# Retention and two feed-forward layers on one core: chunk loads issued by ScalarE, x of two visits in one buffer and one store, drains in the preparation's buffers

## The chip, the core and the metric

The kernel runs on one core of a Trainium2 chip. TensorE (PE) multiplies matrices, VectorE (DVE) and ScalarE (ACT) do the elementwise work, SyncE (SP) issues the transfers (DMAs) between the memory of the chip (DRAM) and the core's own memory. The metric is the time of one execution on the device in microseconds (us), as a median of several runs.

## What is computed

Retention is attention without softmax: the scores are multiplied by a decay per head and masked to earlier positions. Its result x (2304 tokens, 512 wide) passes through two feed-forward layers of width 2048, the first with softplus, the second with a squared ReLU. All is float32.

```python
scores = scale * np.matmul(q, k.transpose(0, 1, 3, 2))
Dmat = np.where(rel >= 0, gamma[:, None, None] ** rel[None, :, :], 0.0)
x = np.matmul(scores * Dmat[None], v)            # 4 x 8 heads x 576 x 64
x = x.transpose(0, 2, 1, 3).reshape(2304, 512)
h = x @ moe_w_in                                  # first layer
x = (np.maximum(h, 0) + np.log1p(np.exp(-np.abs(h)))) @ moe_w_out
r = np.maximum(x @ moe2_w_in, 0)                  # second layer
out = (r * r) @ moe2_w_out
```

## The kernel before, in words

**Numbers as two halves.** A float32 number is split into a rounded part and the rest (names ending in h and l: `gh` and `gl`, `xh` and `xl`), and a product is made of three matrix products of such parts. So every operand costs ScalarE a cast and VectorE a subtraction.

**Stages.** The first layer handles three tiles of tokens, of 512, 384 and 384 (tile 0, 1 and 2, up to token 1280), in 16 steps each; then the other 1024 tokens in one block by Strassen's scheme (lines 1015 and 1148), then the whole second layer by the same scheme (lines 697 and 770) up to the end of the kernel. The change is in the tiles and in the drains.

**A step** (`step`, one of 16 blocks f of the hidden width) does, in this order: g1, 12 matmuls into a PSUM bank `ph` (line 558); Softplus of the bank on ScalarE into `e` (line 569); one or more visits of the retention (`attend`, in tiles 1 and 2 one per step for as long as there are visits); the split of the step before (`split_g`: `gh` on ScalarE, `gl` on VectorE, lines 576 and 577); the rest of the visit (`rest`, called `later()` in `step`); g2 of the step before that, 12 matmuls into four `acc` banks (line 592); then a share of the preparation of the second layer's weights (`pump_step`).

**A visit** works on 64 tokens. Two visits (s = 0 and 1) share a chunk c, which lies in one of the two halves of the buffer `ring`: q and k (0.5 MB), and k and v by tokens (0.5 MB). TensorE makes the scores `pb` of the new chunk (line 426), the outputs `po` of the old one (line 474) and the running state `st` (line 451). VectorE masks `pb` into the ring (line 436) and scales v (line 407), ScalarE copies the state (line 462), VectorE scales `po` into x (line 505 for the tiles, line 497 for tokens from 1280 on).

**The loads of chunks.** `visit` with s = 1 frees one half of the ring: the outputs of the old chunk c - 1 are its last readers. `load_chunk(c + 1)` then issues two DMAs (line 397), first q and k, then k and v. The visit of the next step needs q and k of that chunk for its scores. All these loads, the weights' loads (lines 141 and 146), the stores of prepared weights (`s2d`, line 237), of the first layer's weights (`wod`, line 1581), of x (`x1d`, line 500) and of the results (`x2d`, line 603) stand in one row on SyncE's queue, in the order of the program, and each waits there for what it reads or overwrites.

**Buffers.** Tag `l` of the pool `ew` has two buffers, shared by x of tokens from 1280 on, by two of the four copies of a drain (`drain_one` with odd j, on VectorE) and later by other values. Tag `ct` of the pool `cvt` has six buffers; the preparation writes its words and halves there and stores them from there, and the other two copies of a drain (on ScalarE) take them too. A drain copies the four `acc` banks after the last step of a tile, and stores them.

Up to the end of the tiles the order of the instructions on each engine is that of the program; behind it a scheduler orders them. The result of a visit, x, is 128 x 256 values, 128 KB.

Of the kernel before, what the change touches and what calls it, by code (L numbers as in the profile page):

```python
# [7 lines left out]
F32 = mybir.dt.float32  # L8
# [4 lines left out]
ALU = mybir.AluOpType  # L13
# [3 lines left out]
P = 128  # L17
D = 64
CN = 64
# [9 lines left out]
BLOCK = 1280  # L29
# [25 lines left out]
def kernel(  # L55
# [26 lines left out]
    nc = tc.nc  # L82
# [6 lines left out]
    KD = DM // P  # L89
# [10 lines left out]
    cvt = ctx.enter_context(tc.tile_pool(name="cvt", bufs=6))  # L100
    xs = ctx.enter_context(tc.tile_pool(name="xs", bufs=1))
    ew = ctx.enter_context(tc.tile_pool(name="ew", bufs=2))
# [25 lines left out]
    x1d = dram.tile([2 * FULL // CN, P, KD * CN], F32, name="x1d")  # L128
# [227 lines left out]
    def pump_begin(upto):  # L356
        while n_split[0] < min(n_one, upto):
# [6 lines left out]
            n_used[0] += count  # L364
            begun.append(made)

    x_raw = {}
    chunk = {}
    xop = {}
# [11 lines left out]
    def tile_of(token):  # L381
        for t, (t0, n) in enumerate(TILES):
            if t0 <= token < t0 + n:
                return t, token - t0
        raise ValueError(token)
# [3 lines left out]
    def new_chunk(c):  # L389
        s = c % LOADS * 4  # L390
        chunk[c] = ring[:, s:s + 4].rearrange("p i (h c) -> p i h c", c=CN)

    def load_chunk(c):
        if c < NPR:
            new_chunk(c)
            for i, src in ((0, qk_t), (2, kv)):
                nc.sync.dma_start(
                    out=chunk[c][:, i:i + 2],
                    in_=src[2 * c:2 * c + 2].rearrange("s p i h c -> (s p) i h c"),
                )  # L400

    def scale_v(c):
        if c < NPR:
            t = chunk[c][:, 3]
            m = 2 * c % SCH
            w = vw[:, m * H:(m + 1) * H]
            nc.vector.tensor_tensor(
                out=t, in0=t, in1=w.unsqueeze(2).to_broadcast([P, H, D]), op=ALU.mult
            )
# [6 lines left out]
    def turn(c, s):  # L416
        return (2 * c + s) % SCH, (LO, HI)[s]

    def scores(c, s, pb):
        _, rows = turn(c, s)  # L420
        qp, kk = (chunk[c][rows, i] for i in range(2))
        tos = ((LO, HI), (HI, LO))[s]

        def pair(h):
            for to, hh in zip(tos, (h, h + HH)):
                nc.tensor.matmul(  # L426
                    pb[to, h, :], lhsT=kk[:, hh, :], rhs=qp[:, hh, :],
                    start=True, stop=True, skip_group_check=True,
                )
        return [lambda h=h: pair(h) for h in range(HH)]  # L430


    def masked(c, s, pb):
        _, rows = turn(c, s)
        for i, of in enumerate(((LO, HI), (HI, LO))[s]):
            nc.vector.tensor_tensor(  # L436
                out=chunk[c][rows, 1, i * HH:(i + 1) * HH], in0=pb[of], in1=mask[of], op=ALU.mult
            )

    def states(c, s):  # L440
        m, rows = turn(c, s)
        if m == SCH - 1:
            return []
        if m == 0:
            state[:] = [ps_st.tile([P, HH, D], F32, tag="st", name="st")]
        st = state[0]
        kk, sv = (chunk[c][rows, i] for i in (2, 3))

        def pair(h):
            for to, hh in ((LO, h), (HI, h + HH)):  # L450
                nc.tensor.matmul(
                    st[to, h, :], lhsT=kk[:, hh, :], rhs=sv[:, hh, :],
                    start=m == h == 0, stop=True, skip_group_check=True,
                )
        return [lambda h=h: pair(h) for h in range(HH)]

    def next_state(c, s):
        m, _ = turn(c, s)
        if m < SCH - 1:
            to = (HI, LO)[s]  # L460
            for of, i in ((LO, 0), (HI, 1)):
                nc.scalar.copy(before[to, i * HH:(i + 1) * HH], state[0][of])

    def outputs(c, s, po, carried_first=True):
        m, rows = turn(c, s)
        qp, pp, sv = (chunk[c][rows, i] for i in (0, 1, 3))
        parts = (True, False) if carried_first else (False, True)
        todo = [
            (h, carried) for carried in parts if m or not carried for h in range(0, H, 2)
        ]  # L470

        def pair(n, h, carried):
            for hh in (h, h + 1):
                nc.tensor.matmul(  # L474
                    po[(LO, HI)[hh % 2], hh // 2, :],
                    lhsT=before[rows, hh, :] if carried else sv[:, hh, :],
                    rhs=qp[:, hh, :] if carried else pp[:, hh, :],
                    start=(n == 0), stop=True, skip_group_check=True,
                )
        return [lambda a=a: pair(*a) for a in [(n, *t) for n, t in enumerate(todo)]]  # L480

    def rounds(lower, upper):
        for r in range(max([*lower, *upper, -1]) + 1):
            for half in (lower, upper):
                if r in half:
                    half[r]()

    def at_rounds(*lists):
        return {r0 + r: fn for r0, fns in lists for r, fn in enumerate(fns)}

    def scaled(c, s, po):
        m, _ = turn(c, s)
        token = (2 * c + s) * CN
        xw = cst[:, C_XW + m * 256:C_XW + (m + 1) * 256].rearrange("p (a b) -> p a b", a=KD)
        if token >= BLOCK:
            x = ew.tile([P, 512], F32, tag="l", name="x")[:, :KD * CN]
            nc.vector.tensor_tensor(
                out=x.rearrange("p (a b) -> p a b", a=KD), in0=po, in1=xw, op=ALU.mult
            )
            nc.sync.dma_start(out=x1d[(token - BLOCK) // CN], in_=x)  # L500
            return
        t, off = tile_of(token)
        if t not in x_raw:
            x_raw[t] = xs.tile([P, 512 // CN, KD, CN], F32, tag="xr", name="xr")
        nc.vector.tensor_tensor(out=x_raw[t][:, off // CN], in0=po, in1=xw, op=ALU.mult)
# [29 lines left out]
    def h_bank(name, turn=True):  # L535
        t = ps_h.tile([P, 512], F32, tag=f"h{n_h[0] % 2}", name=name)
        n_h[0] += turn
        return t

    def in_heads(t):  # L540
        return t.rearrange("p (h c) -> p h c", c=CN)
# [54 lines left out]
    def drain_one(j, src, dst, n):  # L596
        if j % 2 == 0:
            o = cvt.tile([P, 512], F32, tag="ct", name="xo")[:, :n]
            nc.scalar.copy(o, src[:, :n])
        else:  # L600
            o = ew.tile([P, 512], F32, tag="l", name="xo")[:, :n]
            nc.vector.tensor_copy(o, src[:, :n])  # L602
        nc.sync.dma_start(out=dst, in_=o)


    def drain(t0, n):
        for j in range(KD):
            drain_one(j, acc[j], x2d[j, :, t0:t0 + n], n)
# [319 lines left out]
    KB = KH * FULL  # L928
    PRODUCT_S = {1: 0, 3: 1, 4: 2, 6: 3}
    t1 = {}  # L930
    full = {}

    def full_raw(i, j):
        return ring.rearrange("p i n -> p (i n)")[:, (2 * i + j) * KB:(2 * i + j + 1) * KB]
# [456 lines left out]
    with tc.manual_schedule():  # L1391
# [12 lines left out]
        for c in range(2, last):  # L1404
            early_qk(c)
            early_kv(c)
        pump_load(3)
        load_chunk(last)
        nc.vector.memset(causal[LO, CN:], 1.0)
        nc.vector.memset(causal[HI, :CN], 0.0)  # L1410
# [69 lines left out]
    def visit(c, s):  # L1480
        old, new = c - 1 in chunk, c < NPR
        first, then = {}, {}
        if old:
            po = in_heads(ps_at.tile([P, 512], F32, tag="at", name="po"))[:, :HH]
            first = at_rounds((0, outputs(c - 1, s, po)))
        if new:
            if c == last:
                pb = in_heads(ps_at.tile([P, 512], F32, tag="at", name="pb"))[:, :HH]
            else:
                pb = in_heads(h_bank("pb", False))[:, :HH]  # L1490
            then = at_rounds((4, scores(c, 1 - s, pb)))
        if s == 0:
            if old:
                then.update(at_rounds((0, states(c - 1, 1))))
            rounds(first, then)
        else:
            if new:
                then.update(at_rounds((0, states(c, 0))))
            rounds(then, first)
        if s and old:  # L1500
            load_chunk(c + 1)
        if new:
            masked(c, 1 - s, pb)

        def rest():
            if s == 0 and old:
                next_state(c - 1, 1)
            elif s and new:
                next_state(c, 0)
            if old:  # L1510
                scaled(c - 1, s, po)
            if s == 0:
                scale_v(c)
            elif old:
                del chunk[c - 1]
        return rest
# [9 lines left out]
    def attend(b, f):  # L1526
        rest = None
        while tick[0] < visits(b, f):
            if rest:
                rest()  # L1530
            rest = visit(*divmod(tick[0], 2))
            tick[0] += 1
        return rest
# [11 lines left out]
    def step(j):  # L1545
# [23 lines left out]
        if j == 0:  # L1569
            load_chunk(last + 1)  # L1570
# [114 lines left out]
```

## Time and profile before

| | before |
|---|---|
| median of 3 runs (lowest, highest) | 831.34 us (831.02, 831.78) |
| the profiled execution, its own time | 830.39 us |
| its span, first to last instruction | 828.6 us |
| granted TensorE clock over the span | 0.994 |
| busy PE, DVE, ACT | 806.9, 653.4, 402.8 us |
| DMA issues of ring loads, line 397 | 14 of each half, 512 KB each |
| DMAs through ScalarE's queue (q10) | 0.09 MB of 202 MB |

Tiles 1 and 2 run from about 125 to about 300 us; visits end near 257 us. Views of the profile: the waits of an engine (who ended its idle time), the timeline (single instructions; "SPq" is an issue of a DMA by SyncE, "ACTq" by ScalarE), the chain that ended last, and windows (busy time, granted clock and transfers of a stretch). Idle time of an engine that nobody waits for costs nothing.

### The profile page before, as it was taken

To read this page: it belongs to the slowest core of one execution; us is meant where nothing else is said; L and a number is where in the kernel's file an instruction comes from. 1 tells how busy PE (TensorE), PEld (TensorE's weight loads), DVE (VectorE), ACT (ScalarE), POOL (GpSimd) and SP (SyncE) were. 2 spreads that over 40 slices of the span, in tenths; PEclk is the share of its full clock that TensorE was granted. 3 is DMA by queue.
4 is the path that set the end of the run, shared out by engine and by line. 5 is a ranking of instruction groups with operands and counts; after the bars stand their busy time and mean duration, and the time that the engine had idled before them with its cause. 6 is when DMAs were issued, how large, how long until landed. Compare 5 with 4: busy or idle time off the path is not lost.

```text
span 828.6 us, 16334 instructions
## 1 busy us (share of the span) xinstructions
PE 806.9 (97%) x5909; PEld 716.1 (86%) x5909; DVE 653.4 (79%) x1255; ACT 402.8 (49%) x781; POOL 0.2 (0%) x4
## 2 busy tenths in 40 slices
PE   8899999989889999999999999999999999999998
PEld 5678889978879997888888899988999988999887
DVE  4899885665755899977778698999797997787876
ACT  3888874543433565556666411464221554111553
POOL 0000000000000000000000000000000000000000
PEclk9999999999999999999999999999999999999999
DMA  9867765898856673327999887898987888877885
GB/s 228 280 185 229 229 217 160 272 317 246 287 188 220 197 233 123 96 83 276 290 330 305 288 285 251 260 311 286 298 252 247 250 271 278 284 250 249 253 272 172
DMA packets 129747, 201.97 MB, mean 244 GB/s; under 512 B 11010, under 2 KB 73090, under 8 KB 128898
## 3 DMA queue, kind: packets, MB, share of 16 engines
q1 hardware_dynamic: 129504, 200.85, 75.7%
q8 instruction: 47, 0.77, 0.4%
q14 instruction: 32, 0.26, 0.1%
q10 hardware_dynamic: 164, 0.09, 0.1%
HBM read 153.71 MB, written 47.19 MB: 242 GB/s over the span
## 4 chain that ended last, share of the span: by engine, by line
PE 80%; DMA 10%; DVE 5%; ACT 2%; issue 1%; SPq 1%; DVEq 0%; ACTq 0%
PE acc L1148 10%; PE acc L592 9%; PE py L770 9%; PE py L697 9%; PE ph L558 9%; PE pz L770 6%; PE px L770 6%; PE pz L697 6%; PE px L697 6%; DMA ring<-in_qk_t_dram 3%; PE py L1015 3%; PE pz L1015 2%; PE px L1015 2%; DMA wi_raw<-in_moe_w_in_dram 2%; PE po L474 1%
## 5 line engine op out<-in xcount | busy, mean ns | idle before, releaser
L592 PE MATMUL acc<-gh,wo 128*128 128x384 f32 (+1 forms) x384 | 118.1, 368 | 1.1 <-DVE xo L602 1.1
L697 PE MATMUL py<-t,sring 128*128 128x384 f32 x432 | 88.4, 339 | 0.7 <-DVE uring L901 0.7
L558 PE MATMUL ph<-xh,wi 128*128 128x384 f32 (+1 forms) x376 | 81.0, 357 | 2.9 <-DVE ring L436 1.5
L592 PEld LDWEIGHTS acc<-gh,wo 128*128 128x128 f32 x384 | 72.5, 192 | 8.8 <-DVE xo L602 1.4
L697 PEld LDWEIGHTS py<-t,sring 128*128 128x128 f32 x432 | 74.9, 188 | 3.7 <-DVE uring L901 1.8
L558 PEld LDWEIGHTS ph<-xh,wi 128*128 128x128 f32 x376 | 68.5, 191 | 8.7 <-issue 1.8
L592 PE MATMUL acc<-gl,wo 128*128 128x384 f32 (+1 forms) x192 | 69.3, 361 | 0.8 <-DVE gl L577 0.8
L718 DVE TENSOR_TENSOR gring<-g,gring 128x384 fp32r<-128x384 f32 (+1 forms) x100 | 57.2, 575 | 12.0 <-ACT gring L750 7.3
L750 ACT CAST gh<-g 128x384 fp32r<-128x384 f32 x84 | 43.2, 515 | 46.7 <-PE px L770 16.3
L718 DVE TENSOR_TENSOR gl<-g,gh 128x384 fp32r<-128x384 f32 (+1 forms) x100 | 57.4, 576 | 9.6 <-ACT gh L750 7.7
L750 ACT CAST gring<-g 128x384 fp32r<-128x384 f32 x84 | 43.3, 516 | 40.1 <-PE py L770 16.4
L697 PE MATMUL pz<-t,sring 128*128 128x384 f32 x288 | 58.9, 335 | 0.0
L697 PE MATMUL px<-t,sring 128*128 128x384 f32 x288 | 58.3, 335 | 0.0
L436 DVE TENSOR_TENSOR ring<-pb,cst 64x256 f32<-64x256 f32 x56 | 23.6, 422 | 42.4 <-PE pb L426 27.7
L569 ACT ACTIVATE e<-ph 128x384 f32<-128x384 f32 (+1 forms) x48 | 25.2, 525 | 64.2 <-PE ph L558 63.9
L897 ACT COPY uring<-px 128x384 f32<-128x384 f32 x24 | 11.5, 480 | 87.8 <-PE px L697 87.8
L718 DVE TENSOR_TENSOR g<-g 128x384 f32<-128x384 f32 x96 | 52.5, 554 | 1.4
L234 ACT CAST ct<-ct 128x512 fp32r<-128x512 f32 (+1 forms) x64 | 35.8, 564 | 35.0 <-DVE ct L258 12.2
L697 PEld LDWEIGHTS px<-t,sring 128*128 128x128 f32 x288 | 50.5, 188 | 0.6 <-ACT uring L897 0.5
L697 PEld LDWEIGHTS pz<-t,sring 128*128 128x128 f32 x288 | 50.8, 188 | 0.1
L235 DVE TENSOR_TENSOR ct<-ct 128x512 fp32r<-128x512 f32 (+1 forms) x64 | 39.2, 621 | 9.5 <-ACT ct L234 6.4
L1148 PE MATMUL acc<-gring,wo 128*128 128x512 f32 x192 | 44.8, 389 | 0.0
(155 smaller groups left out, 1748.5 us busy)
## 6 DMA issues: line engine op xcount, KB each, us to landing
sring<-s2d SPq DMA_DIRECT2D x168, 256.0 KB, 3.2
sring<-o2d SPq DMA_DIRECT2D x168, 256.0 KB, 3.5
wi_raw<-in_moe_w_in_dram SPq DMA_DIRECT2D x32, 512.0 KB, 4.6
wo_raw<-in_moe_w_out_dram SPq DMA_DIRECT2D x32, 512.0 KB, 4.3
s2d<-ct SPq DMA_DIRECT2D x48, 256.0 KB, 4.2
o2d<-ct SPq DMA_DIRECT2D x48, 256.0 KB, 3.3
ring<-in_qk_t_dram SPq DMA_DIRECT2D x14, 512.0 KB, 5.4
ring<-in_kv_dram SPq DMA_DIRECT2D x14, 512.0 KB, 6.4
```

What stands on the lines that cost most here:

```text
L234: nc.scalar.copy(h, src)
L235: nc.vector.tensor_tensor(out=l, in0=src, in1=h, op=ALU.subtract)
L436: nc.vector.tensor_tensor(out=chunk[c][rows, 1, i * HH:(i + 1) * HH], in0=pb[of], in1=mask[of], op=ALU.mult)
L558: nc.tensor.matmul(ph[:, :n], lhsT=a, rhs=x, start=(j == 0), stop=(j == len(todo) - 1))
L569: nc.scalar.activation(out=g, in_=hps.pop(key)[:, :n], func=AF.Softplus)
L592: nc.tensor.matmul(acc[j][:, :n], lhsT=a, rhs=x, start=(begin and m == 0), stop=(end and m == 2))
L697: nc.tensor.matmul(ps, lhsT=a, rhs=x, start=(first and m == 0), stop=(m == len(todo) - 1), skip_group_check=True,)
L718: nc.vector.tensor_tensor(out=out, in0=a, in1=b, op=ALU.subtract)
L750: nc.scalar.copy(h, src)
L770: nc.tensor.matmul(blocks[m][:, :cols], lhsT=a[:, c], rhs=x, start=(first and p == n == 0), stop=(p == NP - 1 and n == len(todo) - 1), ski ...
L1015: nc.tensor.matmul(ps, lhsT=a, rhs=x, start=(first and m == 0), stop=(m == len(todo) - 1), skip_group_check=True,)
L1148: nc.tensor.matmul(accs[half][j], lhsT=a[:, c], rhs=x, start=(begin and m == 0), stop=(end and m == 2),)
```

## The change

1. `load_chunk` takes the queue as an argument. In `visit` the call moves from behind the visit's matmuls to the head of `rest`, with `nc.scalar`: these loads (12 chunks, 24 DMAs) are issued by ScalarE, behind `gh` of the split and ahead of the copies of the state. The loads ahead of the tiles and the one in step 0 stay on SyncE.
2. x of the two visits of a chunk lies in one buffer of 128 x 2 x 256, and is stored by one DMA of 256 KB after the second visit, in place of two of 128 KB.
3. The odd copies of a drain take a buffer of `ct` in place of one of `l`.

```diff
-    def load_chunk(c):
+    def load_chunk(c, queue=nc.sync):
         if c < NPR:
             new_chunk(c)
             for i, src in ((0, qk_t), (2, kv)):
-                nc.sync.dma_start(
+                queue.dma_start(
...
         if token >= BLOCK:
-            x = ew.tile([P, 512], F32, tag="l", name="x")[:, :KD * CN]
+            if s == 0:
+                full["x"] = ew.tile([P, 2, KD * CN], F32, tag="l", name="x")
+            x = full["x"]
             nc.vector.tensor_tensor(
-                out=x.rearrange("p (a b) -> p a b", a=KD), in0=po, in1=xw, op=ALU.mult
+                out=x[:, s].rearrange("p (a b) -> p a b", a=KD), in0=po, in1=xw, op=ALU.mult
             )
-            nc.sync.dma_start(out=x1d[(token - BLOCK) // CN], in_=x)
+            if s:
+                m = (token - BLOCK) // CN - 1
+                nc.sync.dma_start(out=x1d[m:m + 2].rearrange("m p x -> p m x"), in_=x)
             return
...
         else:
-            o = ew.tile([P, 512], F32, tag="l", name="xo")[:, :n]
+            o = cvt.tile([P, 512], F32, tag="ct", name="xo")[:, :n]
             nc.vector.tensor_copy(o, src[:, :n])
...
-        if s and old:
-            load_chunk(c + 1)
         if new:
             masked(c, 1 - s, pb)
         def rest():
+            if s and old:
+                load_chunk(c + 1, nc.scalar)
             if s == 0 and old:
                 next_state(c - 1, 1)
```

In the order of SyncE, a stretch of tile 1 with the pair of ring loads issued from 178.43 us on (the next pair follows behind the last row); before:

```order
L500 DMA x1d<-x 128x256
L237 DMA s2d<-ct 128x2x256 x4
L1581 DMA wod<-wo_697 128x512
L397 DMA ring<-in_qk_t_dram 128x1024
L397 DMA ring<-in_kv_dram 128x1024
L500 DMA x1d<-x 128x256
L141 DMA wi_raw<-in_moe_w_in_dram 128x4x256
L1581 DMA wod<-wo_697 128x512
L500 DMA x1d<-x 128x256
L141 DMA wi_raw<-in_moe_w_in_dram 128x4x256
L237 DMA s2d<-ct 128x2x256 x2
L1581 DMA wod<-wo_697 128x512
```

The same stretch of SyncE after the change (line numbers are 4 or 5 higher there):

```order
L237 DMA s2d<-ct 128x2x256 x4
L1585 DMA wod<-wo_697 128x512
L505 DMA x1d<-x 128x2x256
L141 DMA wi_raw<-in_moe_w_in_dram 128x4x256
L1585 DMA wod<-wo_697 128x512
L141 DMA wi_raw<-in_moe_w_in_dram 128x4x256
L237 DMA s2d<-ct 128x2x256 x2
L1585 DMA wod<-wo_697 128x512
```

The ring loads are gone from SyncE, and the stores of x, one behind each visit, have become one per chunk, twice as large, behind the second visit.

In the order of ScalarE, the step around 176 us, before (`e` is Softplus, `ct` the preparation's casts, `ring<-st` the copies of the state):

```order
L234 CAST ct<-ct 128x512 x2
L569 ACTIVATE e<-ph 128x384
L576 CAST gh<-e 128x384
L462 COPY ring<-st 64x256 x2
L171 ACTIVATE wi_raw<-wi_raw 128x512
L172 ACTIVATE wi_raw<-wi_raw,cst 128x512
```

The same step of ScalarE after the change:

```order
L234 CAST ct<-ct 128x512 x2
L574 ACTIVATE e<-ph 128x384
L581 CAST gh<-e 128x384
L398 DMA ring<-in_qk_t_dram 128x1024
L398 DMA ring<-in_kv_dram 128x1024
L463 COPY ring<-st 64x256 x2
L171 ACTIVATE wi_raw<-wi_raw 128x512
L172 ACTIVATE wi_raw<-wi_raw,cst 128x512
```

The two loads stand behind the two casts of the preparation, Softplus and the cast to `gh`, and ahead of the copies of the state.

## Rows read from the trace of the kernel before

**Rows 1.** Waits of TensorE, 136 to 262 us: total us, times, longest us:
```profile
PE pb L426 <- DMA ring<-in_qk_t_dram: 7.6, 4, 2.7
PE ph L558 <- DVE ring L436: 1.5, 1, 1.5
PE acc L592 <- DVE xo L602: 1.1, 1, 1.1
```

**Rows 2.** Timeline of ScalarE, four Softplus: start, us, what, idle before and its releaser:
```profile
146.62 0.49 ACT L569 ACTIVATE e<-ph 128x384 f32<-128x384 f32 x1 [2.00 <-PE ph L558]
...
235.34 0.49 ACT L569 ACTIVATE e<-ph 128x384 f32<-128x384 f32 x1 [0.92 <-PE ph L558]
...
245.38 0.49 ACT L569 ACTIVATE e<-ph 128x384 f32<-128x384 f32 x1 [4.17 <-PE ph L558]
...
250.84 0.49 ACT L569 ACTIVATE e<-ph 128x384 f32<-128x384 f32 x1 [3.36 <-PE ph L558]
```

**Rows 3.** Windows: stretch, us, busy PE PEld DVE ACT POOL, PEclk, DMA share, GB/s:
```profile
196.80:200.20 3.40, 3.33 (x35) 3.25 (x36) 2.13 (x5) 0.00 (x1) 0.00 (x0) 0.50 0.68 250
241.20:244.60 3.40, 3.01 (x10) 3.04 (x11) 3.33 (x7) 0.00 (x1) 0.00 (x0) 0.51 0.78 237
```

**Rows 4.** Timeline of TensorE: last of a visit, and the next visit where it waited:
```profile
176.39 0.22 PE L474 MATMUL po<-ring 64*64 64x64 f32 x2
...
183.67 0.27 PE L426 MATMUL pb<-ring 64*64 64x64 f32 x2 [1.96 <-DMA ring<-in_qk_t_dram]
```

**Rows 5.** Chain of waits, its ring loads: issue, us to landing, what:
```profile
164.44 5.96 DMA ring<-in_qk_t_dram
178.43 5.20 DMA ring<-in_qk_t_dram
190.35 6.38 DMA ring<-in_qk_t_dram
217.63 5.54 DMA ring<-in_qk_t_dram
```

**Rows 6.** Timeline of SyncE ahead of the load of 178.43:
```profile
175.08 2.71 SPq L237 DMA_DIRECT2D s2d<-ct  x4
```

**Rows 7.** Timeline of TensorE: last of two other visits with late loads:
```profile
189.48 0.34 PE L474 MATMUL po<-ring 64*64 64x64 f32 x6
...
215.18 0.22 PE L474 MATMUL po<-ring 64*64 64x64 f32 x2
```

**Rows 8.** Timeline of ScalarE in the visits of 176 and 215 us:
```profile
175.35 0.62 ACT L234 CAST ct<-ct 128x512 fp32r<-128x512 f32 x1 [0.30 <-DVE ct L260]
176.38 0.51 ACT L576 CAST gh<-e 128x384 fp32r<-128x384 f32 x1
...
215.41 0.50 ACT L576 CAST gh<-e 128x384 fp32r<-128x384 f32 x1
```

**Rows 9.** Line 397, the ring loads: issue ns min/median/max, and us to landing:
```profile
L397 SPq DMA_DIRECT2D ring<-in_qk_t_dram x14: 328/343/2476, 15.4 to 231.0; - x14
...
DMA to landing us min/median/max: 3.3/6.0/10.6
```

**Rows 10.** Line 1397, DMAs that ScalarE issues: issue ns min/median/max:
```profile
L1397 ACTq DMA_DIRECT2D cst<-in_consts_dram x2: 554/582/611, 0.7 to 1.3; - x2
```

**Rows 11.** Windows of the stretch with ring loads, and of a full one:
```profile
164.40:231.00 66.60, 58.97 (x849) 55.23 (x850) 41.20 (x86) 28.46 (x63) 0.00 (x0) 0.95 0.85 273
166.00:175.00 9.00, 8.00 (x102) 7.55 (x101) 6.20 (x14) 2.49 (x6) 0.00 (x0) 1.00 1.01 351
```

**Rows 12.** Timeline of VectorE around 222 us:
```profile
221.94 0.69 DVE L235 TENSOR_TENSOR ct<-ct 128x512 fp32r<-128x512 f32 x1 [0.41 <-ACT ct L234]
223.95 0.43 DVE L436 TENSOR_TENSOR ring<-pb,cst 64x256 f32<-64x256 f32 x1 [1.32 <-PE pb L426]
```

**Rows 13.** Timeline of SyncE and VectorE at the drain of the second tile:
```profile
232.90 0.33 SPq L500 DMA_DIRECT2D x1d<-x  x1
...
238.67 0.56 DVE L602 COPY xo<-acc 128x384 f32<-128x384 f32 x1 [5.34 <-DMA x1d<-x]
```

More of the change, by code (lines that the diff above doesn't have):

```diff
@@ L365, in pump_begin @@
             begun.append(made)
+    full = {}
     x_raw = {}
@@ L930 @@
     t1 = {}
-    full = {}
     def full_raw(i, j):
```

## The prediction

> **What bounds the kernel now.** I read the engines' shares first: TensorE is busy for 806.9 of 828.6 us, so only its idle time and its slow time can be won. Its waits between 136 and 262 us come next [rows 1]: 7.6 us in four waits of scores `pb` for a ring load, 1.1 us for a drain's copy `xo`, 1.5 us for a mask `ring` that VectorE had not made yet. Then I looked at how steps follow each other, because a stall costs more than its idle time. ScalarE starts Softplus when `ph` is done, so in a step without a stall the distance of two such starts is the step: 250.84 - 245.38 = 5.46 us [rows 2]. From 146.62 to 245.38 us there are 15 steps in 98.76 us, where 15 x 5.46 = 81.90 would do: 16.86 us are lost. The step from 235.34 to 245.38 alone, that of the drain, takes 10.04 us, 4.58 more than a quiet one; the other 12.28 us belong to the ring loads.
>
> Of the 16.86 us, 10.2 are the waits of [rows 1]. The granted clock gives the next part: in three stretches of 3.4 us, the first and the last of which are shown, it is 0.50, the lower of the two levels, 1.2 GHz [rows 3]; half of 3 x 3.4 is 5.1 us. They begin behind a ring wait, behind the longest ring wait, and behind the two waits of the drain. The stall of 1.96 us before 183.67 us [rows 4] has no such stretch behind it. The last 1.6 us I put down to the refilling of the pipeline behind stalls.
>
> **Why the ring loads are late.** Take the load of 178.43 us. The outputs that free its half of the ring end at 176.39 + 0.22 = 176.61 us, and TensorE is ready for the new scores at 183.67 - 1.96 = 181.71 us [rows 4]: a load has 5.10 us from the last output to its landing. It took 5.20 us, was issued 1.82 us late [rows 5], and TensorE waited 1.96. It was late because SyncE worked through four stores and one more ahead of it, from 175.08 us on [rows 6]. The load of 217.63 us came 2.23 us behind its last output at 215.40, that of 190.35 us 0.53 behind 189.82 [rows 5, 7]. The load of 164.44 us was issued in time and took 5.96 us: transfers issued before it were still under way. The shortest ring load took 3.3 us [rows 9], which shows what a load needs when little lies ahead of it.
>
> **The change part by part.** *Loads on ScalarE.* Twelve chunks, 24 DMAs, leave SyncE. ScalarE reaches them behind `gh`. At 215 us `gh` ends at 215.91, so the issue comes about 0.5 us behind the last output, in place of 2.23; at 190 us it comes at once, in place of 0.53. At 176 us it is different: ScalarE's cast `ct` of 175.35 us waits for work of VectorE and writes a buffer whose store has to land, Softplus and `gh` follow and end at 176.89 us [rows 8]. With no stall before it TensorE would be there 1.3 us earlier, ScalarE not: I take the issue as 1.5 us late and a stall of 1.4 us that stays.
>
> The issue itself takes 0.34 us on SyncE in the median [rows 9] and 0.55 to 0.61 us where ScalarE issues now [rows 10]; two per chunk hold ScalarE for 0.7 to 1.2 us. Behind them wait the copies of the state, needed one step later, and the preparation. ScalarE is busy for 28.5 of 66.6 us in this stretch [rows 11] and idles 1 to 4 us before a Softplus [rows 2], so this costs nothing; without that cover it would be 0.7 to 1.2 us per chunk, 8 to 14 us for twelve.
>
> How long the loads take on a queue of their own no row shows, since ScalarE moves no large transfer before. The bounds are the rows of the ring loads: 3.3 us, with which no stall is left, and 6.38 us [rows 5, 9]. I take 4.7 us, about the middle. That leaves the 1.4 us at 176 us, about 0.4 us at the other loads together, and nothing that lowers the clock.
>
> The Trainium skill, "DMA: Bandwidth & Descriptors", section "Queues, rings and completion order", says that each DMA engine takes turns between the queues that have work for it, packet by packet. By this rule a load would pass most of what lies ahead on SyncE's queue; no row of the trace before shows it.
>
> *Cover that is late next.* From 221.94 to 222.63 us VectorE makes a half `ct`, and the mask of the visit, two of 0.43 us, comes behind it [rows 12]. Without the stall the new scores start at 215.40 + 5.10 = 220.5 and end some 0.4 us later; g1 of the next step writes the same bank behind g2, which is about 2.1 us of the 5.46 us step: at 223.0 us. The mask is done at 222.63 + 0.86 = 223.5, so TensorE waits about 0.5 us: 0.6 us stay with refilling.
>
> *Transfers.* From 164.4 to 231.0 us 273 GB/s are moved in 66.6 us, 18.2 MB [rows 11]. These are ten steps, 54.6 us without stalls: 333 GB/s, against 351 in one of the fullest stretches, where the DMA engines are busy throughout [rows 11]. So the stage comes near what the transfers can do. At 351 GB/s it fits; at 300 GB/s it would take 60.7 us, 6 us more. I take 2.0 us, and 0 and 6 as ends.
>
> *One store for two visits.* Eight stores of 256 KB replace sixteen of 128 KB; eight issues of 0.33 us [rows 13] leave SyncE, which nobody on the path waits for. The second visit's x now stands in a buffer that was already taken for the first, so VectorE waits for a store half as often. I cost it at nothing.
>
> *Drains in `ct`.* VectorE's copy `xo` waited 5.34 us for the store of x, issued at 232.90 us, and VectorE's masks stood behind it [rows 13]. With six `ct` buffers, whose last stores stand well ahead of the drain on SyncE, the copies find room. The preparation's next words wait for the drain's stores instead; these need 5.8 us if they land like that store of x (238.67 - 232.90), about when, a step later, the words are due. I keep 0.3 of 4.58 us. The scheduler orders the block behind the tiles a little differently on VectorE and ScalarE; I cost that at 0, with 1 us either way.
>
> **Sum.** Lost 16.86; still lost afterwards 1.4 + 0.4 + 0.6 + 2.0 + 0.3 = 4.7; gain 12.2. From the profiled execution's 830.4 us that gives 818.2; the median of the runs stands 0.95 above that execution, so 819.1 us.
>
> **Rivals.** *A: only the late issue is won.* If transfers take as long as before, the loads stall by their length plus lateness less 5.10: 0.9 (5.96), 1.4 (6.38 with 0.1), 1.0 (5.54 with 0.5), and at 176 us 5.20 with 1.5, 1.6; 4.9 us, with a share of refilling 5.7, perhaps one slow-clock stretch of 1.7, and the 0.6, 2.0 and 0.3 from above: 10.3 stay, gain 6.6, 824.8 us. For it: all DMAs share the same engines, full in the critical 5 us. Against it: loads that had little ahead of them took 3.3 us.
>
> The Trainium skill, same page, section "Issuing engines are not separate DMA queues", speaks for this rival: issuing from several engines saves only the time of the issue. By it the result is 824.8 us.
>
> *B: ScalarE holds the loads back, slower.* Behind its own order, with casts that wait for stores to land, ScalarE could be late at every chunk as it is at 176 us. With eight stalls of 2.2 us, 17.6 us, and four stretches of half clock at 1.7, 24.4 us stand against the 12.28 of now; less 4.3 from the drain that is 7.8 us more, 839.1 us. It decides from about 2 us on, where eight stalls alone (16.6 / 8) use up both gains. For it: the one visit at 176 us. Against it: `gh` ends within 0.5 us of the last output at 215 us, and ScalarE mostly waits for TensorE.
>
> *C: transfers bind.* At 300 GB/s 6 us of the stage stay in place of 2, and preparation that is late makes VectorE and ScalarE late at two or three more masks, some 3 us: gain 12.2 - 4 - 3 = 5.2, 826.1 us.
>
> *D: no change.* The stalls move elsewhere one for one, 831 us. Nothing in the rows speaks for it.
>
> **How the numbers follow.** Forecast 0.55, A 0.22, C 0.09, D 0.05, B 0.09. The predicted time is that of the forecast, 819.1 us. Its own range goes from 814.5 (all 16.86 won) to 823; with A and most of C the range is 814.4 to 828.0 us. A measurement of this kernel tells about 0.2% from no change. Faster by more: forecast, A and C, 0.86; within: 0.05; slower: 0.09.
>
> **What would show it.** Waits of `pb` for ring loads fall from 7.6 to about 2 us; one of them, about 1.4 us, remains near 178 us, behind an issue that comes late on ScalarE. Ring loads through ScalarE's queue take 4 to 5 us. No stretch of half clock is left between 190 and 245 us. The copy `xo` no longer waits for x. Fifteen steps from the second of tile 1 on take about 87 us in place of 98.8. Wrong I am if the loads still take 5.5 us and more, if ScalarE's `gh` ends behind the last output by 1.5 us at several chunks, or if `xo` or `ct` wait for stores instead.

## The result and the profile after

The changed kernel takes 821.3 us in the median of four runs (819.63 to 824.67) against 831.2; the ratio is 0.988, its 95% interval 0.985 to 0.990. Forecast were 819.1 us and a range from 814.4 to 828.0. The profiled execution took 819.63 us where 818.2 was forecast, 10.76 us less than that of before.

TensorE's waits between 136 and 262 us, for [rows 1]; columns: who waited for what, us in total, times, longest:

```profile
PE pb L427 <- DMA ring<-in_qk_t_dram: 5.4, 4, 2.0
PE ph L563 <- DVE ring L437: 0.9, 1, 0.9
```

Ring waits fell from 7.6 to 5.4 us only. The wait for the drain's copy and the wait of 1.5 us for a mask behind it are gone; the 0.9 us is another mask, the one that the prediction looked for near 222 us. TensorE's timeline:

```profile
222.88 1.30 PE L563 MATMUL ph<-xh,wi 128*128 128x384 f32 x6 [0.85 <-DVE ring L437]
```

ScalarE's timeline, its Softplus starts, for [rows 2]:

```profile
146.64 0.49 ACT L574 ACTIVATE e<-ph 128x384 f32<-128x384 f32 x1 [0.83 <-PE ph L563]
...
225.32 0.49 ACT L574 ACTIVATE e<-ph 128x384 f32<-128x384 f32 x1 [1.53 <-PE ph L563]
230.72 0.49 ACT L574 ACTIVATE e<-ph 128x384 f32<-128x384 f32 x1 [0.58 <-PE ph L563]
236.18 0.49 ACT L574 ACTIVATE e<-ph 128x384 f32<-128x384 f32 x1 [1.77 <-PE ph L563]
```

The drain's step, 230.72 to 236.18, is 5.46 us, a quiet step to the hundredth. The 15 steps take 236.18 - 146.64 = 89.54 us, 9.22 less than before; the other 1.5 us were won behind the tiles. Against 15 quiet steps 7.64 us are still lost. Windows of the stretch of ten steps (columns as in [rows 3]), for the first of [rows 11]:

```profile
164.40:226.41 62.01, 57.35 (x915) 53.20 (x915) 41.59 (x86) 29.59 (x64) 0.00 (x0) 1.00 0.88 294
```

The granted clock is 1.00 throughout, where it was 0.95, and the 18.2 MB pass in 62.0 us in place of 66.6. The chain of waits still has three ring loads (issue, us to landing), for [rows 5]; below it the issues of the ring loads on ScalarE (ns min/median/max), for [rows 9, 10]:

```profile
142.27 6.47 DMA ring<-in_qk_t_dram
...
165.93 6.92 DMA ring<-in_qk_t_dram
...
189.99 6.16 DMA ring<-in_qk_t_dram
```

```profile
L398 ACTq DMA_DIRECT2D ring<-in_qk_t_dram x12: 334/335/392, 74.6 to 226.4; - x12
L398 ACTq DMA_DIRECT2D ring<-in_kv_dram x12: 444/483/1232, 75.0 to 226.8; - x12
```

The wait behind the first of the three is new (first row, TensorE's timeline). The kernel before issued this load at 142.24 us, and TensorE did not wait for it (second row, its chain of waits):

```profile
148.78 0.33 PE L427 MATMUL pb<-ring 64*64 64x64 f32 x4 [1.62 <-DMA ring<-in_qk_t_dram]
...
142.24 5.00 DMA ring<-in_qk_t_dram
```

Whether the queue made it longer is looked at under parts 2 and 3 alone.

From 90 us on none of the loads was issued later than 0.1 us behind the last output, but two of the three took longer than any ring load of [rows 5]. What lay ahead of the load of 165.93 us shows in SyncE's timeline (first fence) and in the DMA queues' share of the 1.98 us behind its issue, of the next 2.09 us, and of the 0.99 us behind the issue of the load of 155.01 us, which landed after 3.3 us (second fence: queue, packets, MB, share; q1 is SyncE's, q10 ScalarE's):

```profile
164.22 0.37 SPq L141 DMA_DIRECT2D wi_raw<-in_moe_w_in_dram  x1
164.65 0.50 SPq L1585 DMA_DIRECT2D wod<-wo  x1
```

```profile
q1 hardware_dynamic: 527, 0.61, 97.6%
...
q10 hardware_dynamic: 138, 0.54, 84.0%
q1 hardware_dynamic: 59, 0.09, 22.2%
...
q1 hardware_dynamic: 10, 0.02, 4.4%
```

For two microseconds after the issue only bytes that SyncE had issued before move, 0.61 MB. The first of the two is the delay of an issue: with next to nothing ahead ScalarE's packets start after about 1 us. In the second none of them moves either. Later both queues move side by side: from 170.0 to 172.9 us, just before the load lands, they share the engines like this,

```profile
q1 hardware_dynamic: 517, 0.51, 52.3%
q10 hardware_dynamic: 144, 0.49, 46.2%
```

and SyncE's part is work that it issued from 167.80 us on, behind the load. "DMA: Bandwidth & Descriptors" of the Trainium skill, section "Queues, rings and completion order", has the engines take turns between queues packet by packet. The stretch from 170.0 to 172.9 us fits this; in the second microsecond behind the issue no packet of ScalarE's queue got a turn.

So the bytes ahead are not the whole length. The load of 202.05 us had as much ahead of it, three stores of 256 KB, and landed after 5.0 us without a wait (SyncE's timeline, and the load's KB and us to landing):

```profile
200.53 1.59 SPq L237 DMA_DIRECT2D s2d<-ct  x3
...
ring<-in_qk_t_dram ACTq DMA_DIRECT2D x1, 512.0 KB, 5.0
```

What makes the difference, the kind of transfer ahead or what SyncE issues behind, no run takes apart.

The drain's odd copies, VectorE's timeline, for [rows 13]; they wait for nothing:

```profile
228.17 1.03 DVE L607 COPY xo<-acc 128x384 f32<-128x384 f32 x2
```

### The profile page after: what moved, and what is told of

Same layout as the page of the kernel before. It is cut to its first block, busy times and chain, and to the rows that moved or that the text cites. A ratio compares the mean times of both kernels' runs of the same rounds, so it can differ in the third digit from the quotient of the medians.

```text
span 817.8 us, 16322 instructions
## 1 busy us (share of the span) xinstructions
PE 801.8 (98%) x5909; PEld 712.2 (87%) x5909; DVE 653.5 (80%) x1255; ACT 402.5 (49%) x781; POOL 0.2 (0%) x4
## 4 chain that ended last, share of the span: by engine, by line
PE 89%; DMA 6%; DVE 2%; ACT 1%; issue 1%; SPq 1%; DVEq 0%; ACTq 0%
PE acc L597 12%; PE ph L563 11%; PE acc L1152 11%; PE py L702 9%; PE py L775 9%; PE px L702 6%; PE pz L775 6%; PE px L775 6%; PE pz L702 6%; PE py L1019 4%; PE px L1019 3%; PE pz L1019 2%; DMA ring<-in_qk_t_dram 2%; PE po L475 2%; DMA qk<-in_qk_t_dram 1%; PE pb L427 1%
## 5 line engine op out<-in xcount | busy, mean ns | idle before, releaser
L597 PE MATMUL acc<-gh,wo 128*128 128x384 f32 (+1 forms) x384 | 115.9, 363 | 0.0
L597 PEld LDWEIGHTS acc<-gh,wo 128*128 128x128 f32 x384 | 70.8, 188 | 7.3 <-ACT gh L581 0.4
```

The source lines that it names most:

```text
L597: nc.tensor.matmul(acc[j][:, :n], lhsT=a, rhs=x, start=(begin and m == 0), stop=(end and m == 2))
```

## The experiments

Theory M: a ring load lands when the bytes that were issued ahead of it, on whichever queue, are through; a queue of its own saves the lateness of the issue and nothing more. Its rivals are a delay that belongs to ScalarE's queue, and the mere fullness of the DMA engines. Ratios are to the kernel before on the same chip, whose runs there spread from 828 to 838 us, more than the 0.2% that the prediction took for the noise. Waits are totals of TensorE's ring waits in one profiled execution, 136 to 262 us. That execution need not be a typical one: those of parts 2 and 3 alone (829.4 us), of the doubled stores (826.4) and of the last row (818.7) were the slowest of their kernels, that of the moved stores (818.2) the fastest of its four.

| kernel | ratio, 95% interval | ring waits us |
|---|---|---|
| the change | 0.988 (0.985 to 0.990) | 5.4 |
| the change, again | 0.987 (0.983 to 0.990) | 4.9 |
| part 1 alone | 0.993 (0.990 to 0.995) | 6.0 |
| parts 2 and 3 alone | 0.992 (0.989 to 0.994) | 10.6 |
| part 2 alone | 1.003 (1.001 to 1.005) | 10.8 |
| part 3 alone | 0.993 (0.990 to 0.995) | 8.0 |
| first half of q, k first | 0.989 (0.983 to 0.995) | 4.0 |
| weight stores out of tile 1 | 0.987 (0.981 to 0.992) | 2.1 |
| weight stores doubled | 0.990 (0.985 to 0.994) | 7.3 |
| 512 KB loads behind ring loads | 0.980 (0.977 to 0.983) | 0.2 |
| that, weight stores moved too | 0.980 (0.976 to 0.983) | 0 |
| that order, on SyncE | 0.989 (0.987 to 0.991) | 2.9 |
| that order, without part 2 | 0.980 (0.977 to 0.983) | 1.0 |

**Part 1 alone.** The drain copies and x of the kernel before, with

```diff
-        if s and old:
-            load_chunk(c + 1)
...
         def rest():
+            if s and old:
+                load_chunk(c + 1, nc.scalar)
```

> Part 1 alone: the chunk loads are issued by ScalarE in `rest`, x and the drains are as before. Theory S (the two gains are separate): the drain keeps its step of about 10 us with the 4.6 us lost there, the half clock behind it and the two waits; the ring part gives what it gave in the changed kernel, 11 - 4.6 = 6 us or so: 825 us. Rival T (the parts need each other: without the free buffers VectorE's copies and masks come late and the loads gain nothing, or the x stores in their old place lengthen the loads): under 3 us gained, 828 to 831.

825.1 us against 832.4. The ring waits are about those of the full change, and the drain's stall stands as before: VectorE's copy waits for the store of x, and half clock follows (first window). A second stretch of half clock stands behind the first ring wait, 1.65 us (second window), where the changed kernel's profile has none behind 1.62 us.

```profile
236.64 0.56 DVE L602 COPY xo<-acc 128x384 f32<-128x384 f32 x1 [5.58 <-DMA x1d<-x]
```

```profile
238.80:242.20 3.40, 2.66 (x9) 2.67 (x9) 3.32 (x8) 0.38 (x1) 0.00 (x0) 0.50 0.68 202
149.40:152.80 3.40, 3.40 (x12) 3.40 (x12) 3.29 (x8) 0.00 (x0) 0.00 (x0) 0.50 0.86 304
```

**Parts 2 and 3 alone.** The two edits above undone in the changed kernel.

> Parts 2 and 3 alone: one x store for two visits, drains in `ct`, chunk loads on SyncE at the old place. Theory S: the drain's step falls from 10.0 to about 5.5 us, ring waits stay at about 7.8 us, with the two half-clock stretches behind them: 831.2 - 4.6 = 826.5 us. Rival T: the store of x in one piece already shortens SyncE's row ahead of the loads at 178 and 217 us, so that the loads are issued earlier and these parts alone win 7 us or more, 824 or less.

825.3 us against 832.4, 0.8%. The parts add up, as theory S says: 0.7 and 0.8% make 1.6%, the whole had 1.2 to 1.3%; the difference is within the intervals. The gain of 7.1 us is more than the 4.6 of theory S, and by the time alone rival T would stand; but its early issue does not show: in this kernel the load near 180 us still goes out behind SyncE's four stores, and the waits are 10.6 us, against 7.8 expected.

This kernel also shows what the queue does to a load that is issued in time. Two of its ring loads, on SyncE's queue, issued 0.1 us behind the last output (chain of waits):

```profile
142.37 6.52 DMA ring<-in_qk_t_dram
167.63 7.03 DMA ring<-in_qk_t_dram
```

On ScalarE's queue the same two took 6.47 and 6.92 us. So the new wait before 148.78 us is not the queue's doing: on SyncE's queue, too, this load took from 5.00 us (the kernel before) to 6.52 us.

**Part 2 alone, part 3 alone.** From the kernel before, only the diff's second part, and only its third.

> Part 2 alone: x of two visits in one buffer and one store; ring loads on SyncE at the old place, the drain's odd copies in `l` as before. Theory D (the drain's gain is that its copies don't wait for a store of x): the copy `xo` still waits some 5 us for the store of x, now of 256 KB, the drain's step keeps its 10 us; SyncE's row ahead of two loads is shorter by one issue of 0.33 us: ratio 0.996 to 1.002. Rival X (fewer stores shorten SyncE's row enough to bring the loads in time): ratio 0.990 to 0.994.

> Part 3 alone: the drain's odd copies take a `ct` buffer; all else as before. Theory D: the drain's 4.6 us are won here, `xo` does not wait, ring waits stay at 7.8 us or a little more: ratio 0.992 to 0.995. Rival X: the store of x is needed for it, since `x` itself waits for the buffers: under 2 us, ratio 0.997 to 1.000.

Part 3 brings the gain of the drain, 0.75%. Part 2 alone is slower by 0.3%, just beyond theory D's range; why is not shown. The copy still waits for the store of x (first row, of part 2 alone: idle time of `xo` and its releaser), and the ring waits of that execution are longer (second row).

```profile
  DMA x1d<-x: 5.6, 1
...
PE pb L427 <- DMA ring<-in_qk_t_dram: 10.8, 5, 3.3
```

**Half of q and k first.** In the changed kernel, on ScalarE:

```diff
+                for s, rows in ((1, HI), (0, LO)):
+                    queue.dma_start(out=chunk[c][rows, 0:2], in_=qk_t[2 * c + s])
```

> The changed kernel, but ScalarE issues a chunk's q and k as two loads of 256 KB, first the 64 partitions that the next visit's scores read, then the other 64, then k and v. Theory M (a load takes long because its bytes share the DMA engines with what SyncE has in flight): the first half lands after its first 2 us of start plus half of the 4 to 4.7 us of transfer, 4 to 4.6 us in place of 5 to 6.9, the four ring waits of 5.4 us together fall under 1 us: 821 - 4.5 to 5.5, about 816. Rival L (the length is a delay that doesn't depend on the bytes): the waits stay within 1 us of 5.4 and the time within 1 us of 821. Rival N (64 partitions reach only part of the DMA engines or of the ports): the first half takes as long as the whole load, no gain, and a third issue of 0.34 us on ScalarE: 821 to 823.

The half that the scores read, 256 KB issued at 166.77 us, landed after 7.3 us, and TensorE waited 2.4 us:

```profile
  PE pb L433: 2.4, 1
...
DMA to landing us min/median/max: 7.3/7.3/7.3
```

Halving a load's own bytes bought next to nothing there; my expectation from theory M, 4 to 4.6 us, was wrong. The 7.3 us are not like for like with the 6.92 of the whole load: SyncE's 512 KB load went out at 165.80 us here, 0.97 us ahead, and 1.71 us ahead in the changed kernel. Counted from the issue of that load the half landed after 8.29 us, the whole after 8.63. Alone this run could not tell the rivals L and N from that.

**Fewer and more bytes on SyncE.** The stores of the first layer's weights, one of 256 KB per step of tile 1, are moved, and in another kernel doubled:

```diff
-        g, i = divmod((b - 1) * KF + f, 4)
-        if 0 <= g <= G_GROUP:
+        outs = []
+        if b == 0 and f >= 4:
+            outs = [f - 4]
+        elif b == last_b and f < 6:
+            outs = [12 + 2 * f, 13 + 2 * f]
+        for g, i in (divmod(m, 4) for m in outs):
```

```diff
+            if b == 1:
+                nc.sync.dma_start(out=wo2[g][:, i * DM:(i + 1) * DM], in_=words_out[:, i])
```

> The changed kernel, but the 24 stores of the first layer's weights (256 KB each), of which one goes out in every step of tile 1, are moved: 12 into tile 0, 12 into the first six steps of tile 2. In the stretch of the ring loads SyncE then moves 256 KB less in every step of 5.5 us. Theory M: the loads that take 6 to 7 us fall by the time of those 256 KB where they are in flight, 0.7 us at 350 GB/s, the four waits from 5.4 to about 2.5 to 3 us, 821 to about 818.5; unless the doubled stores of tile 0 or 2 delay something there. Rival L: lengths and waits as in the changed kernel, 821.

> The changed kernel, but in tile 1 each of the 16 stores of 256 KB of the first layer's weights is done twice (the second time to a place nobody reads), so SyncE moves 256 KB more per step of 5.5 us. Theory M: every ring load with such bytes ahead grows by 0.7 us or more (256 KB at 350 GB/s), the four waits of 5.4 us become 8 or more and some of the loads without a wait get one; with a stretch of half clock behind a wait of 2 us or more 4 to 8 us slower than the changed kernel, ratio to before 0.992 to 0.998. Rival L (a fixed delay of ScalarE's queue): waits as in the changed kernel, ratio 0.988, unless the DMA engines run full and the preparation itself comes late.

The waits go with the bytes on the other queue: 2.1 us without these stores, 4.9 to 5.4 with them, 7.3 with twice as many, where 8 or more were expected. A fixed delay of ScalarE's queue would have left them alone. These are single executions, a fast one and a slow one at the ends, so the direction counts more than the sizes. In time, the doubled kernel is 825.4 us against 822.4 of the change on the same chip, with overlapping intervals, and its ratio is better than the 0.992 to 0.998 expected; the thinned one cannot be told from the change by its ratio.

**The same bytes in another order.** The one 512 KB load of raw weights that SyncE issues just ahead of every second ring load is held back and issued by ScalarE right behind it:

```diff
+            if s and old:
                 load_chunk(c + 1, nc.scalar)
+                release(nc.scalar)
...
+        held[0] = b == 1 and not ends and tick[0] % 2 == 1
```

`held` makes the preparation count the load in place of issuing it; `release` issues what was counted. In the changed kernel the four loads of this kind go out at 140.60, 164.22, 188.37 and 211.74 us, and the four ring loads behind them are the four that TensorE waits for in its profile.

> The changed kernel, but the one 512 KB load of raw weights that SyncE issues some 1.7 us ahead of every second ring load of tile 1 (four in all) is issued by ScalarE right behind that ring load. Bytes moved are the same. Theory M (a ring load waits for the bytes that were issued ahead of it, on whichever queue): the four ring loads that wait fall from 6 to 7 us to between 3.5 and 5, their waits from 5.4 to about 1 us: 4 to 5 us faster than the changed kernel, ratio to before about 0.982. Rival A' (what counts is how full the DMA engines are over the stretch, not the order): the waits stay at 4 to 6 us, ratio 0.988. Rival P (the preparation needs those loads at once): ring waits fall, but VectorE and ScalarE wait for the weights and hand the time back, ratio 0.986 to 0.99.

> The changed kernel once more, on the chip of the next three, so that they can be compared with it: 0.9877 of the kernel before, four ring waits of 5.4 us together, no half clock. All theories expect the same.

816.3 us against 822.4 for the change: 6.0 us. Fullness is not the cause: the ten steps move 304 GB/s here against 294, and the ring waits are all but gone. More moved than the 512 KB: on SyncE the store `wod` of 256 KB stood behind each of these loads. With the load held it no longer waits for it, and the one of 164.65 us goes out 5 us earlier, together with the store ahead of it:

```profile
158.96 0.96 SPq L1599 DMA_DIRECT2D wod<-wo  x2
```

It is the same at the load of 142 us. So the 6.0 us belong to both, the load and the store behind it. Waits (first fence) and the ten steps (second):

```profile
PE ph L574 <- DVE ring L448: 2.1, 2, 1.9
PE pb L438 <- ACT ring L474: 0.9, 1, 0.9
PE pb L438 <- DMA ring<-in_qk_t_dram: 0.2, 1, 0.2
```

```profile
164.38:222.81 58.43, 55.45 (x849) 51.59 (x850) 41.49 (x86) 28.58 (x62) 0.00 (x0) 1.00 0.95 304
```

The stall that is left is the one I had looked for at 176 us. ScalarE's and TensorE's timelines there:

```profile
176.15 0.62 ACT L234 CAST ct<-ct 128x512 fp32r<-128x512 f32 x1 [5.85 <-DMA s2d<-ct]
177.12 0.62 ACT L234 CAST ct<-ct 128x512 fp32r<-128x512 f32 x1 [0.35 <-DMA s2d<-ct]
177.25 0.34 ACTq L409 DMA_DIRECT2D ring<-in_qk_t_dram  x1
...
177.76 0.49 ACT L585 ACTIVATE e<-ph 128x384 f32<-128x384 f32 x1
```

```profile
174.99 0.22 PE L486 MATMUL po<-ring 64*64 64x64 f32 x2
...
179.37 1.65 PE L574 MATMUL ph<-xh,wi 128*128 128x384 f32 x8 [1.87 <-DVE ring L448]
```

The casts wait for stores to land, and the load goes out 2.04 us behind the last output (175.21). TensorE waits here for VectorE's mask, which stands behind the same casts.

**Both orders, and the queue.** The moved loads and the moved weight stores together; and the moved loads with `load_chunk(c + 1)` and `release(nc.sync)`.

> Both: the 512 KB loads behind the ring loads, and the 24 stores of the first layer's weights moved out of tile 1. Theory M: no ring wait over 0.5 us is left, about 1 us better than the better of the two, ratio to before about 0.980 to 0.981. Rival A': thin_wod's gain alone, two or three waits of 2 us together, ratio about 0.985.

> The kernel with the 512 KB loads behind the ring loads (ratio 0.980 to before), but the ring loads, and those loads behind them, are issued by SyncE in place of ScalarE, in that order. Theory I (part 1 of the change is worth the time of the issue: four stores that SyncE issues one after the other still stand ahead of the loads near 178 and 215 us): the loads that had nothing ahead stay without a wait, those two are issued about 2 us late and TensorE waits 1.5 to 3.5 us at each, with a stretch of half clock behind one of them: 5 to 8 us slower than with ScalarE, ratio 0.986 to 0.990. Rival O (once the order of the bytes is right the queue doesn't matter): ratio 0.979 to 0.982.

Together 815.6 us; no ring wait is left, but it cannot be told from 816.3. On SyncE the same order takes 821.4 us, 5.0 us more by the medians and 0.9% (7 us) more by the ratios, as theory I has it. For the loads with nothing ahead TensorE does not wait; those behind SyncE's stores go out late, and the two ring waits, 0.75 and 2.14 us, stand behind them. They are shorter than the 1.5 to 3.5 us of theory I, but the profile has two stretches of half clock in place of its one. SyncE's timeline:

```profile
176.30 2.18 SPq L237 DMA_DIRECT2D s2d<-ct  x4
178.54 0.49 SPq L1599 DMA_DIRECT2D wod<-wo  x1
179.12 0.60 SPq L409 DMA_DIRECT2D ring<-in_qk_t_dram  x1
...
198.86 4.25 SPq L237 DMA_DIRECT2D s2d<-ct  x3
203.16 0.46 SPq L1599 DMA_DIRECT2D wod<-wo  x1
203.72 0.40 SPq L409 DMA_DIRECT2D ring<-in_qk_t_dram  x1
```

The second place was near 204 us and not near 215, as I had it.

**Without part 2.** The 512 KB loads behind the ring loads, x stored after each visit again.

> The kernel with the 512 KB loads behind the ring loads on ScalarE (ratio 0.980 to before), without part 2: x is stored after each visit again, 128 KB at a time. Theory N (with the loads on ScalarE nobody on the path waits for SyncE's stores of x, so part 2 is worth nothing): ratio 0.978 to 0.982, the waits of TensorE as there. Rival Y (the larger store, ahead of or beside the ring loads, lengthens them, as part 2 alone with ring waits of 10.8 us and a ratio of 1.003 may say): ring loads are shorter, ratio 0.976 to 0.978. Rival Z (two stores more per chunk make SyncE's row or the `l` buffers bind): ratio 0.983 or more.

814.9 us, ratio 0.980: theory N. With the ring loads on ScalarE part 2 is worth nothing that shows. That its loss alone came through the loads on SyncE's queue is likely, but not shown. Three versions between 814.9 and 816.3 us beat both kernels; they cannot be told apart.

## Why the prediction was right, and where its terms were not

**Right: what bounds, and the drain.** A stall costs its idle time and the half clock behind it. The drain's step came back whole: forecast 0.3 us left, measured 0. No half clock is left in 164 to 226 us, as forecast. That is in part luck: part 1 alone had it behind a ring wait no longer than those that stayed here, and the slowest of the four runs, 824.67 us, has a mean clock of 0.997 where the profiled one has 0.999; a stretch of 3.4 us at half clock takes about 0.002 off the mean (an estimate, 1.7 of 818 us). Part 3 alone shows that the free buffer did it.

**Right: the late issue.** The ring loads of the changed kernel go out at once. The better order on SyncE, late again at two places, costs 0.9%. ScalarE's issues took 0.33 to 1.23 us, and in the changed kernel no wait of TensorE stands behind them.

**Mis-sized: "How long the loads take on a queue of their own".** I took 4.7 us, the middle of two bounds; the three in the chain took 6.16 to 6.92, two of them beyond the upper end of 6.38, and all beyond the 5.5 us that I had named as a sign of being wrong. The step that failed is that a load on its own queue would pass what SyncE has in flight; on SyncE's queue, issued in time, two of these loads took as long (6.52 and 7.03 us, parts 2 and 3 alone). I had the right picture in rival A, and the Trainium skill's sentence for it ("DMA: Bandwidth & Descriptors", "Issuing engines are not separate DMA queues"): only the time of the issue is saved. Rival A has 4.9 us of ring waits. Waits of 5.43 us stood where 1.4 + 0.4 were forecast, 3.6 us too many.

**The place at 176 us.** I expected ScalarE late there "with no stall before it". A stall of 1.96 us at 170.94 us stayed, TensorE came later itself, and the load of 179.13 us was in time. Where the stall before it is gone, ScalarE is late by 2.04 us, more than the 1.5 forecast, but the mask's wait covers it. The mask near 222 us cost 0.85 us, forecast 0.6.

**Too dear: transfers.** I let 2.0 us stay because 333 GB/s would be needed. Of the 7.64 us that the 15 steps still lose, 5.43 and 0.85 are waits; 1.36 is left for refilling and transfers together. With the loads in another order the ten steps run in 58.4 us at 304 GB/s, 3.8 more than quiet, of which the waits are 3.0 (1.87, 0.87 and 0.23). That leaves 0.9 us for refilling and for the sum of the transfers there, though these ten steps move slightly less, 17.8 MB. What the transfers cost beyond that, they cost through the order in which they land.

**The sum.** Left in the steps: 7.64 in place of 4.7, 2.9 too little forecast. Behind the tiles 1.54 us were won for which I had costed 0 with 1 either way: 1.2 of it lies in the first half of the block (line 1019), which begins 9.2 us earlier than before (292.67 us) and ends 10.4 us earlier (374.46). It takes 83.0 us before and 83.6 with part 2 alone, but 82.0 with part 1 alone and 81.5 with part 3 alone, so either of these two brings it; how, stays open. So 818.2 became 819.6. That this is near is in part luck: 3.6 us of ring waits were missing from the sum, and the 1.5 us behind the tiles and the transfers, taken too dear, made up for more than half of them. For the ring loads rival A has the mechanism; its 824.8 us was missed because its half clock and its share of transfers did not come and the 1.54 us did.

**Part 2 at nothing:** right beside loads on ScalarE, tested in the kernel with the moved order; alone it is 0.3% slower.

## What to carry to other kernels

When a wait is for a DMA, ask first what was issued just ahead of it on any queue: moving a 512 KB load, four times, behind the load that TensorE needs next bought 6.0 us, together with the store that this freed to go out earlier; splitting the needed load bought nothing that shows. Another engine's queue was worth the time by which the old engine issues late, 5 to 7 us here, and nothing more that these runs show. Before a length is put down to a queue, look at the same load in other executions: one load took 5.00 us in one kernel and 6.52 us in another, both times on SyncE's queue. Between far-apart bounds of a transfer's length, go by the row with the same traffic ahead of it, not by the middle.

## What the runs showed of the hardware

A load on ScalarE's queue moved no packet for 1.98 us while 0.61 MB of SyncE's moved, and started after about 1 us where SyncE had next to nothing in flight. It landed after 6.92 us; the same load, issued in time on SyncE's queue (parts 2 and 3 alone), after 7.03. With three stores of 256 KB ahead in place of a load and a store, about the same bytes, a load landed after 5.03 us.

A DMA issue on ScalarE does not wait for the end of the work ahead of it. In the kernel with the 512 KB loads moved, the issue of 177.25 us began while the cast of 177.12 us still ran until 177.74; in the changed kernel that of 179.13 us ran beside a `gh` that ended at 179.52. It does stay in the order of ScalarE: the first went out 0.13 us behind the start of that cast, which had waited for a store. The prediction had placed the issues behind the end of `gh`, 0.5 us late at 215 us; they went out 0.1 us behind the last output.
